# Turning gathered rows by TensorE in halves of 64 rows instead of blocks of 128

## The chip, the cores and the metric

One core of one Trainium2 chip runs the whole program. The metric is the device time of one execution in microseconds (us), lower is better; the time quoted for a kernel is the median of its runs. A profile of one execution stands beside the times. Its engines are PE (TensorE matmul), PEld (TensorE loading its stationary operand), DVE (VectorE), ACT (ScalarE), POOL (GpSimd) and SP (SyncE, which issues DMAs).

## The reference

Two stages in float32. The first is an attention of 8 batches of 8 heads, 576 positions, head size 64: a coarse attention over averages of 4 positions, repeated 4 times, plus a local attention in a band of 7 positions. Its output is laid out as 4608 tokens of 512 values. The second is a mixture of 8 experts with one expert for each token:

```python
def _moe_ref(x, modality_id, w_gate, modality_bias, w1, w2):
    logits = x @ w_gate + modality_bias[modality_id]      # x: 4608 x 512
    e_idx = np.argmax(logits, axis=1)
    ...                                                   # gate_w: softmax value of the chosen expert
    for e in range(8):
        mask = e_idx == e
        h = np.maximum(x[mask] @ w1[e], 0.0)              # 512 -> 1024
        out[mask] = gate_w[mask, None] * (h @ w2[e])      # 1024 -> 512
```

## The kernel before, in words

**Attention and routing.** The first part computes attention in an order written out by hand (a table of phases), stores the tokens' rows to a scratch tensor `xs` in HBM, and writes each token's number into a table `tab` sorted by expert. It fills about the first 260 us and the change doesn't touch it.

**Units of work.** The second part goes over a list `order` of units. A unit is up to 512 slots of one expert: blocks of 128 rows, H of them. There are two early units (H = 4, number 0 and 1, already prepared during the attention), six more of H = 4, one of H = 2, one of H = 1 and one of H = 2: 37 blocks in all. A loop for whatever is left (`For_i`) runs zero times with this data.

**What one unit does.** `gather` fetches the unit's rows from `xs` by indirect DMAs on POOL's queue into a buffer `R` (tile `xg`, 128 rows x 512 values for each block; two buffers in turn). `xsplit` turns each block: four transposes on TensorE, each of 128 rows x 128 columns against an identity matrix, fill one bank of PSUM (tile `xt`, tag `"T"`, three banks for all users of that tag). ACT then copies the bank to `xh` in the rounded matmul format, and DVE subtracts `xh` from the bank to get the remainder `xl`. `compute` runs the first layer as products of three kinds (`wh*xh`, `wh*xl`, `wl*xh`) on L886 and splits the hidden values into `hh` and `hl` on ACT and DVE; `second` runs the second layer block by block on L934, scales on ACT (L937) and scatters rows to the output with an indirect DMA on POOL (L938). Weights arrive by SP's queue and are split on ACT (L811) and DVE (L817).

**The order around the change.** `xsplit` is a generator: each `next` issues one step (the transposes of a block, then the copy, then the subtraction). While unit i is in its second layer, `mid(h)` at the head of each block calls `split(i + 1, h)`, which takes three `next` for each block it has to do; `SPLIT[4] = (2, 1, 1)` puts two blocks at the first `mid`, one at the second and one at the third. For unit 0 the steps are placed by hand inside the attention. Outside the hand-written part a scheduler sets the order on each engine: it follows the program's order but lets a later instruction go ahead where it expects an engine to be free. Both `xh` and `xl` have one buffer, so their copies begin only when the first layer of the unit before has read them.

Of the kernel before, what the change touches and what calls it, by code (L numbers as in the profile page):

```python
# [7 lines left out]
F32 = mybir.dt.float32  # L8
# [4 lines left out]
ALU = mybir.AluOpType  # L13
# [4 lines left out]
B, H, S, D = 8, 8, 576, 64  # L18
# [28 lines left out]
TB, SB = 3, 3  # L47
# [708 lines left out]
class Moe:  # L756
# [91 lines left out]
        s.turn["h"] = s.turn.get("h", -1) + 1  # L848
        return [s.xb.tile([128, 8, 512], F32R, name=nm) for nm in ("hh", "hl")]

    def xsplit(s, R, H=2):

        nc, C = s.nc, s.C
        xh = s.we.tile([128, 4, 512], F32R, name="xh")
        xl = s.we.tile([128, 4, 512], F32R, name="xl")
        for h in range(H):
            p = s.ps.tile([128, 4, 128], F32, name="xt", tag="T", bufs=TB)
            for k in range(4):
                nc.tensor.transpose(p[:, k, :], R[:, h, 128 * k : 128 * k + 128], C.ident)
            yield xh, xl  # L860
            hs = slice(128 * h, 128 * h + 128)
            nc.scalar.copy(xh[:, :, hs], p)
            yield
            nc.vector.tensor_tensor(xl[:, :, hs], p, xh[:, :, hs].bitcast(F32), op=ALU.subtract)
            yield
        return xh, xl
# [80 lines left out]
def build(tc, q, k, v, mid, w_gate, bias, w1, w2, out):  # L947
    nc = tc.nc
    with ExitStack() as ctx:
# [3 lines left out]
        ps = ctx.enter_context(tc.tile_pool(name="ps", bufs=2, space=PSUM))  # L953
        xs = dp.tile([NTOK + 1, DM], F32, name="xs")
        tab = dp.tile([NSLOT + CAP, 2], I32, name="tab")
        C = Consts(tc, cp, ps)
        moe = Moe(tc, ctx, C, ps, xs, tab, w1, w2, out)
        with ExitStack() as actx:
# [85 lines left out]
            def piece(key, f, done):  # L1044

                try:
                    next(going[key] if key in going else going.setdefault(key, f()))
                except StopIteration as x:
                    done(x.value)

            def split(u):
                piece(("x", u), lambda: moe.xsplit(E[u][2], 4), E[u].append)

            def wload(c):
                raw.append(moe.wload(E[0][0], c // 4, c % 4))
# [14 lines left out]
            T, R, E, W = {}, {}, {}, []  # L1070
# [28 lines left out]
            for j in range(13):  # L1099
                call(free + 0.4 + 0.15 * j, split, 0)  # L1100
# [65 lines left out]
        for i, (_, _, H) in enumerate(order):  # L1166
            if i == 0:
                with tc.high_priority():
                    lists["p"] = ro.pairs(cnt, moe.xp)
            if i == 1:  # L1170
                lists["m"] = ro.late(cnt, moe.xp)
            if i:
                gather(i + 2)

            def mid(h):
                if i == h == 0:
                    gather(2)
                split(i + 1, h)

            if H == 1:  # L1180
                moe.compute_half(Ts[i], Ws[i], Xs[i], step, mid)
            else:
                moe.compute(Ts[i], Ws[i], Xs[i], H, step, mid)
# [5 lines left out]
        with tc.For_i(0, nu, 1) as iv:  # L1189
# [4 lines left out]
            T = moe.entries(te, 1)  # L1194
            R = moe.gather(T)
# [33 lines left out]
```

## Time and profile before

| | |
|---|---|
| time, median of 3 runs | 715.84 us (709.83 to 716.35) |
| the profiled execution's own time, its span | 716.96 us, 715.3 us |
| PE busy in the span | 662.0 us (93%), 7467 matmuls |
| DVE, ACT, POOL busy | 379.2 us, 358.7 us, 262.9 us |
| granted TensorE clock, mean | 0.974 |
| transposes of `xsplit` (L859) | 148, of 128 x 128 each |

In a row of the profile `xt<-ident,xg 128*128 128x128 f32` means: tile `xt` is written, `ident` streams through TensorE (the moving operand, 128 partitions x 128 columns) and `xg` is held in it (the stationary operand, 128 rows x 128 columns). In a timeline the first number is the start in us from the span's start, the second the time until the last of the merged instructions has ended, and `x12` says how many were merged. Matmuls are pipelined: one begins before the one ahead has ended, so what a matmul costs in a full stream is the distance from its start to the next start, not its duration.

### The profile page before, as it was taken

How to read it: one execution, taken by the hardware profiler on the slowest of the kernel's cores; microseconds unless marked ns; L12 is line 12 of the kernel's file. 1: busy time of each engine (PE TensorE's matmuls, PEld its weight loads, DVE VectorE, ACT ScalarE, POOL GpSimd, SP SyncE). 2: the span in 40 equal slices, each digit the busy share in tenths (PEclk: the TensorE clock that was granted, in tenths of full speed). 3: DMA queues.
4: the chain of work that ended last, by engine and by line, in shares of the span. 5: the costliest groups of instructions: out<-in, count | busy, mean ns of one | idle time of the engine just before them, and what ended most of it. 6: DMA issues, size and time to landing. Idle time of an engine off the chain costs nothing. (4 is left out here: it accounts for less than half of the span.)

```text
span 715.3 us, 19216 instructions
## 1 busy us (share of the span) xinstructions
PE 662.0 (93%) x7467; PEld 535.7 (75%) x7467; DVE 379.2 (53%) x877; ACT 358.7 (50%) x804; POOL 262.9 (37%) x351
## 2 busy tenths in 40 slices
PE   7889999998968798999999999999999999999991
PEld 4677776776746666887888888888888888889790
DVE  3678687787848686836533245333453243525510
ACT  3678777777756574534444234433444234444610
POOL 6756665857647857353030310403103011010200
PEclk9799999999989899999999999999999999999996
DMA  9799799897889757579560744516435154346400
GB/s 178 148 186 173 162 165 181 174 184 130 145 147 214 152 151 186 154 228 294 143 219 21 189 148 116 179 58 190 165 102 156 67 162 148 103 133 186 159 13 29
DMA packets 179439, 107.93 MB, mean 151 GB/s; under 512 B 139309, under 2 KB 157777, under 8 KB 179346
## 3 DMA queue, kind: packets, MB, share of 16 engines
q1 hardware_dynamic: 172274, 87.49, 53.1%
q0 software_dynamic: 7072, 19.18, 8.3%
q8 instruction: 60, 0.98, 0.7%
q14 instruction: 33, 0.27, 0.2%
HBM read 87.39 MB, written 19.51 MB: 149 GB/s over the span
## 5 line engine op out<-in xcount | busy, mean ns | idle before, releaser
L938 POOL DMA_INDIRECT out_dram<-o,tg x37 | 40.9, 1106 | 302.7 <-ACT o L937 245.5
L817 DVE TENSOR_TENSOR wlo<-raw,whi 128x1024 fp32r<-128x1024 f32 x73 | 87.4, 1222 | 84.4 <-ACT whi L811 74.4
L891 DVE SCALAR_TENSOR_TENSOR hl<-l,hh 128x512 fp32r<-128x512 f32 x72 | 49.4, 688 | 101.7 <-ACT hh L890 101.7
L934 PE MATMUL l<-whi,hh 128*128 128x512 f32 x256 | 100.2, 395 | 0.0
L934 PE MATMUL l<-wlo,hh 128*128 128x512 f32 x256 | 99.6, 390 | 0.0
L934 PE MATMUL l<-whi,hl 128*128 128x512 f32 x256 | 99.6, 390 | 0.0
L890 ACT ACTIVATE hh<-l 128x512 fp32r<-128x512 f32 x72 | 42.9, 597 | 110.7 <-PE l L886 109.3
L886 PE MATMUL l<-xh,whi 128*128 128x512 f32 (+1 forms) x256 | 95.0, 374 | 0.4 <-DVE hl L891 0.2
L886 PE MATMUL l<-xh,wlo 128*128 128x512 f32 (+1 forms) x256 | 94.8, 370 | 0.0
L886 PE MATMUL l<-xl,whi 128*128 128x512 f32 (+1 forms) x256 | 94.7, 370 | 0.0
L811 ACT CAST whi<-raw 128x1024 fp32r<-128x1024 f32 x70 | 71.4, 1050 | 28.2 <-DMA raw<-in_moe_w_dram 18.2
L937 ACT ACTIVATE o<-l,tg 128x512 f32<-128x512 f32 x37 | 25.3, 687 | 98.5 <-PE l L934 70.5
L407 ACT COPY Pw<-lt 32x288 f32<-32x288 f32 x128 | 54.6, 426 | 3.2 <-DVE lt L402 1.8
L934 PEld LDWEIGHTS l<-wlo,hh 128*128 128x128 f32 x256 | 48.1, 188 | 10.1
L886 PEld LDWEIGHTS l<-xh,whi 128*128 128x128 f32 x256 | 48.1, 188 | 9.7 <-POOL xg L1063 0.5
L934 PEld LDWEIGHTS l<-whi,hl 128*128 128x128 f32 x256 | 48.1, 188 | 9.5
L934 PEld LDWEIGHTS l<-whi,hh 128*128 128x128 f32 x256 | 48.1, 188 | 9.5
L886 PEld LDWEIGHTS l<-xh,wlo 128*128 128x128 f32 x256 | 48.3, 189 | 8.3
L886 PEld LDWEIGHTS l<-xl,whi 128*128 128x128 f32 x256 | 48.3, 189 | 8.0
L337 PE MATMUL sc<-kT,qT 64*24 64x32 f32 x3072 | 45.5, 195 | 8.1 <-issue 7.4
L391 POOL TENSOR_TENSOR le<-le,zr 128x384 f32<-128x384 f32 x32 | 26.8, 836 | 70.0 <-DVE zr L387 53.5
L337 PEld LDWEIGHTS sc<-kT,qT 64*24 64x24 f32 x3072 | 35.3, 101 | 22.8 <-issue 18.2
(241 smaller groups left out, 1277.9 us busy)
## 6 DMA issues: line engine op xcount, KB each, us to landing
raw<-in_moe_w_dram SPq DMA_DIRECT2D x176, 128.0 KB
raw<-in_moe_w_dram SPq DMA_DIRECT2D x44, 512.0 KB
vw<-in_v_dram SPq DMA_DIRECT2D x53, 192.0 KB
qt<-in_q_dram SPq DMA_DIRECT2D x30, 288.0 KB
kt<-in_k_dram SPq DMA_DIRECT2D x30, 288.0 KB
xs<-R SPq DMA_DIRECT2D x64, 128.0 KB
vw<-in_v_dram SPq DMA_DIRECT2D x15, 96.0 KB
xs<-R SPq DMA_DIRECT2D x12, 64.0 KB
```

What stands on the lines that cost most here:

```text
L337: s.nc.tensor.matmul(p[32 * j : 32 * j + SUB, i, :], qT[r, q0 : q0 + SUB], kT[r, q0 : q0 + WIN], start=False, stop=(i == NB - 1), skip_gro ...
L391: s.nc.gpsimd.tensor_tensor(e, e, z[:, : 2 * NB].unsqueeze(2).broadcast_to([128, 2 * NB, WIN]), op=ALU.mult)
L407: s.nc.scalar.copy(s.Pw[n % NPW][r, :, j, :SUB], s.t["lt", n][r, :, :SUB])
L811: (nc.gpsimd.tensor_copy if turn <= 4 else nc.scalar.copy)(hi, raw)
L817: (nc.gpsimd if turn == 4 else nc.vector).tensor_tensor(lo, raw, hi.bitcast(F32), op=ALU.subtract)
L886: nc.tensor.matmul(p[:, f % n, :], a[:, fs], x[:, k, :N], start=(k == 0 and i == 0), stop=(k == 3 and i == 2))
L890: nc.scalar.activation(hh[:, g, :N], p, AF.Relu)
L891: nc.vector.scalar_tensor_tensor(hl[:, g, :N], p, 0.0, hh[:, g, :N].bitcast(F32), op0=ALU.max, op1=ALU.subtract)
L934: nc.tensor.matmul(p, a[:, f, hs], x[:, f % 2, :], start=(f == 0 and i == 0), stop=(f == 7 and i == 2))
L937: nc.scalar.mul(o, p, T[:, h, 1:2].bitcast(F32))
L938: nc.gpsimd.indirect_dma_start(out=s.out[:, :], out_offset=bass.IndirectOffsetOnAxis(ap=T[:, h, 0:1], axis=0), in_=o, in_offset=None, boun ...
```

## The change

All units but number 0 (which gets `pairs=False`) with an even H take two blocks at a time. Each block is turned in two halves: the lower 64 rows (r = 0) and the upper 64 rows (r = 1), so a transpose has a stationary operand of 64 rows x 128 columns and streams 64 columns of the identity. Sixteen such transposes are issued for the two blocks with lower and upper in turn; all lower halves of both blocks go to one bank of PSUM and all upper halves to another. The copy on ACT and the subtraction on DVE then take one bank each as before, 128 x 512 values, read and written with a stride in runs of 64. The number of steps of the generator for two blocks stays six: all sixteen transposes belong to the first.

```diff
-    def xsplit(s, R, H=2):
+    def xsplit(s, R, H=2, pairs=True):
         nc, C = s.nc, s.C
         xh = s.we.tile([128, 4, 512], F32R, name="xh")
         xl = s.we.tile([128, 4, 512], F32R, name="xl")
+        if pairs and H % 2 == 0:
+            for h in range(0, H, 2):
+                ps = [s.ps.tile([128, 2, 4, 64], F32, name="xt", tag="T", bufs=TB) for r in range(2)]
+                for g in range(2):
+                    for k in range(4):
+                        for r in range(2):
+                            rs = slice(64 * r, 64 * r + 64)
+                            nc.tensor.transpose(ps[r][:, g, k], R[rs, h + g, 128 * k : 128 * k + 128], C.ident[rs, rs])
+                for r in range(2):
+                    yield xh, xl
+                    p = ps[r].rearrange("m g k x -> m k g x")
+                    hi, lo = [x[:, :, 128 * h : 128 * h + 256].rearrange("m k (g r x) -> m k g r x", g=2, r=2)[:, :, :, r]
+                              for x in (xh, xl)]
+                    nc.scalar.copy(hi, p)
+                    yield
+                    nc.vector.tensor_tensor(lo, p, hi.bitcast(F32), op=ALU.subtract)
+                    yield
+            return xh, xl
         for h in range(H):
...
             def split(u):
-                piece(("x", u), lambda: moe.xsplit(E[u][2], 4), E[u].append)
+                piece(("x", u), lambda: moe.xsplit(E[u][2], 4, False), E[u].append)
```

## The prediction, made before the changed kernel was run

> **What bounds the kernel now.** I first read the busy times of the page, then the table of stretches of the expert part, with a cut at the last matmul.
>
> ```profile
> PE 662.0 (93%) x7467; PEld 535.7 (75%) x7467; DVE 379.2 (53%) x877; ACT 358.7 (50%) x804; POOL 262.9 (37%) x351
> ```
> ```profile
> core 0: us, PE busy (x) PEld busy (x) DVE busy (x) ACT busy (x) POOL busy (x), PEclk, DMA share, GB/s
> 284.00:340.00 56.00, 55.45 (x260) 45.47 (x261) 36.04 (x94) 26.14 (x35) 20.43 (x17) 1.00 0.78 230
> 340.00:460.00 120.00, 120.00 (x554) 99.53 (x553) 48.68 (x63) 47.66 (x66) 22.64 (x23) 1.00 0.48 138
> 600.00:699.00 99.00, 97.46 (x530) 84.46 (x529) 38.32 (x43) 38.41 (x52) 11.50 (x10) 1.00 0.38 120
> 699.00:715.30 16.30, 0.64 (x3) 0.19 (x1) 0.00 (x0) 0.69 (x1) 0.98 (x1) 0.58 0.04 16
> ```
>
> From 340 to 460 us PE is busy 120.00 of 120.00 at the full granted clock, while DVE and ACT are at 40%. Over these stretches it is idle for 0.5 to 1.5 us at most; behind the last matmul 16 us of closing work follow that the change doesn't touch. So a nanosecond of PE time added or taken in the second part moves the end by one, and the question is what the transposes cost on PE before and after. Next come the transposes' own line, and the matmuls around one batch.
>
> ```profile
> L859 PEld LDWEIGHTS xt<-ident,xg x148: 137/141/144, 262.5 to 671.6; 128*128 128x128 f32 x148
> L859 PE MATMUL xt<-ident,xg x148: 270/272/330, 262.5 to 671.7; 128*128 128x128 f32 x148
>   POOL xg L838: 7.6, 4
> ```
> ```profile
> 446.66 0.39 PE L934 MATMUL l<-wlo,hh 128*128 128x512 f32 x1
> ...
> 447.34 0.39 PE L934 MATMUL l<-wlo,hh 128*128 128x512 f32 x1
> 447.58 1.47 PE L859 MATMUL xt<-ident,xg 128*128 128x128 f32 x12
> 448.80 0.48 PE L934 MATMUL l<-whi,hh 128*128 128x512 f32 x1
> 449.12 0.40 PE L934 MATMUL l<-whi,hl 128*128 128x512 f32 x1
> ```
>
> Twelve transposes in 1.47 us, the last lasting 0.27: a step of (1.47 - 0.27) / 11 = 0.109 us. Products step by (447.34 - 446.66) / 3 = 0.227. From 447.34 to 449.12 are 1.78 us; less two product steps the batch costs 1.33, that is 12 x 0.109 and 0.02 for entering and leaving. Of the 148 transposes 16 are unit 0's and 4 the one-block unit's; the other 128 cost 128 x 0.109 = 14.0 us. That is all there is to win from.
>
> What sets the 0.109?
>
> ```profile
> 38.06 0.49 PE L413 MATMUL pdt<-ident,de 128*96 128x128 f32 x3
> 441.09 0.49 PE L859 MATMUL xt<-ident,xg 128*128 128x128 f32 x3
> ```
> ```profile
> 38.39 0.22 PEld L274 LDWEIGHTS tp<-ident,qt 128*128 128x128 f32 x2
> 38.39 0.25 PE L328 MATMUL sc<-mask,identb 128*128 128x192 bf16 x1
> 38.47 0.60 PE L274 MATMUL tp<-ident,qt 128*128 128x128 f32 x4
> ```
>
> Three transposes with 96 stationary columns take as long as three with 128, so the 128 streamed columns set the step. And a load of 128 columns that begins with the mask's matmul at 38.39 doesn't hold back its transpose at 38.47: it hides within 0.08 us.
>
> **What the change does to PE.** *Stream.* A half streams 64 columns: 0.109 x 64/128 = 0.055, call it 0.056 us. If the lower and the upper half run side by side, a pair of halves costs 0.056 in place of 0.109. Rows of two matmuls side by side:
>
> ```profile
> L364 PE MATMUL scd<-kd,qd 64*64 64x144 f32 x384 | 31.2, 296 | 0.4 <-POOL pool L112 0.4
> 35.13 0.95 PE L364 MATMUL scd<-kd,qd 64*64 64x144 f32 x12
> ```
>
> Twelve in 0.95 us less 0.28 for the last leave 0.67 us for five steps of two, about 0.12 a step when the entry is taken off; twelve one after the other would need 1.4. Those twelve differ in rows and in columns of the array, while the new halves share the columns. So full overlap isn't shown, and that is a rival below. With it, 128 pairs save 128 x 0.053 = 6.8 us.
>
> *Entering and leaving the half-row shape.* This is what the change adds and the diff doesn't show. Matmuls whose stationary operand has another count of rows or columns stand beside each other in the attention:
>
> ```profile
> 39.34 0.25 PE L328 MATMUL sc<-mask,identb 128*128 128x192 bf16 x1
> 39.52 0.25 PE L180 MATMUL mp<-ident,mf 36*128 36x36 f32 x1
> 39.70 0.29 PE L337 MATMUL sc<-kT,qT 64*24 64x32 f32 x12
> ```
> ```profile
> 270.96 0.96 PE L886 MATMUL l<-xh,whi 128*128 128x512 f32 x3
> 271.85 0.72 PE L442 MATMUL avl<-Pw,vw 128*64 128x96 f32 x12
> 272.50 0.50 PE L886 MATMUL l<-xl,whi 128*128 128x512 f32 x1
> 272.83 0.39 PE L886 MATMUL l<-xh,wlo 128*128 128x512 f32 x1
> ```
>
> The same mask matmul that let a full transpose follow after 0.08 lets the 36-row transpose of L180 follow after 0.18: 0.10 us for a change of rows alone. Into L442 the last product starts at 270.96 + 0.96 - 0.39 = 271.53, and 0.32 follow instead of 0.227: 0.09. Out of it: the last starts at 271.85 + 0.72 - 0.25 = 272.32 and 0.18 follow instead of 0.08, 0.10 again; then 0.33 instead of 0.227, another 0.10, since the first load could not be hidden. On the way in that uncovered load costs 0.06 (330 against 272 ns in L859's row). A run of halves between products thus pays 0.09 + 0.06 + 0.10 + 0.10 = 0.35 us; today's runs pay 0.02; net 0.33. If the loads were hidden after all it would be 0.2, and the sum below +1.2.
>
> The Trainium skill, page "TensorEngine Tiling (Array Packing)", section "Tiling Modes", says that changing the tiling mode drains TensorE. The rows above agree, with 0.10 us at each change; a price it doesn't give.
>
> *How many runs.* Each contiguous run of transposes would pay that. In the trace they stand from the first to the last of these rows in 27 runs, the one-block unit left out:
>
> ```profile
> 284.15 0.63 PE L859 MATMUL xt<-ident,xg 128*128 128x128 f32 x4 [1.84 <-DMA xg<-xs,tg]
> 422.80 0.27 PE L859 MATMUL xt<-ident,xg 128*128 128x128 f32 x1
> 422.82 0.47 PE L886 MATMUL l<-xh,whi 128*128 128x512 f32 x1
> 670.69 0.48 PE L934 MATMUL l<-whi,hh 128*128 128x512 f32 x1
> 671.31 0.66 PE L859 MATMUL xt<-ident,xg 128*128 128x128 f32 x4
> ```
>
> A middle unit has three: one alone as a filler in the first layer (422.80), the rest of that block (441.09), and twelve at 447.58, which are its last block and, two banks ahead, the first two blocks of the next unit. I expect these places again: a filler, the second pair, and the next unit's first pair.
>
> *The banks.* A pair holds two of three banks. The first pair is turned a layer early; so the second finds one bank free, for its lower halves, and the upper ones wait until DVE has subtracted the first pair's bank. Whether that is in time:
>
> ```profile
> 441.20 1.87 DVE L864 TENSOR_TENSOR xl<-xt,xh 128x512 fp32r<-128x512 f32 x3
> 485.46 1.27 DVE L864 TENSOR_TENSOR xl<-xt,xh 128x512 fp32r<-128x512 f32 x2
> 486.48 0.49 PE L859 MATMUL xt<-ident,xg 128*128 128x128 f32 x3
> 531.77 0.60 PE L859 MATMUL xt<-ident,xg 128*128 128x128 f32 x4
> 531.88 1.88 DVE L864 TENSOR_TENSOR xl<-xt,xh 128x512 fp32r<-128x512 f32 x3
> ```
>
> A subtraction takes 0.68, so the bank comes free at 441.88 for a run at 441.09 (late), at 486.14 for 486.48 (in time), at 532.56 for 531.77 (late). Two of three are late; I take four of the seven units of four blocks. There the scheduler issues the lower halves alone, goes on with products and issues the upper ones later: one run more, and 8 pairs with nothing overlapped, which cost 2 x 0.056 against 0.109, as much as today.
>
> *Beside PE.* ACT and DVE keep one instruction for each bank of the same size, in runs of 64. Twice their time would still be covered by the second layer's matmuls (DVE 48.68 of 120 us busy). On POOL's queue `gather` waits for the last transpose that read its buffer (7.6 us in four waits); it moves by the length of a run, and the rows are fetched a unit ahead. Before the last unit's second block (671.31, 0.62 behind a product instead of 0.23) PE already waits 0.4 us and may again.
>
> *Sum.* 31 runs x 0.33 = +10.2; 96 overlapped pairs x 0.053 = -5.1; 32 others +0.1: **+5.2 us**. The profiled execution took 716.96 and would take 722.2; on the median of 715.84, which I forecast, **721.0 us**.
>
> **The rivals.** *All pairs overlap.* The banks are in time, 27 runs: +8.9 - 6.8 = +2.1, 717.9 us; were each of the 16 pairs in one run, 5.3 - 6.8 = -1.5, 714.3. For it: the unit at 486.48. Against it: the two late ones and the fillers.
>
> *The price of the change of shape is not paid.* Then 6.8 us are won: 709.0. Only a missing drain would do it, and the 0.18 ahead of L180, itself a transpose of fewer rows, speaks against it. The Trainium skill, page "TensorE: Matmul & The Clock Gate", section "Part 3: Packing small matmuls", gives the span of packed tiles as one matmul and about 4 ns for each tile more, with no price of entry. By that rule this rival would hold; no run here shows tiles that share columns.
>
> *The halves don't run side by side (slower).* Both need the whole 128 columns of the array. If a half only starts when the other has streamed, pairs cost 0.112 and nothing is won: +0.4 + 10.2 = +10.6, 726.4. If the load of 128 columns also shows, at its bound of 0.08, 256 x 0.08 - 14.0 + 10.2 = +16.7, 732.5. It decides as soon as a pair costs more than 0.08. For it: no row shows two such loads at once. Against it: L364's loads do overlap. The same Trainium skill page, section "LDWEIGHTS (loading the stationary operand)", lets the load's time go with the columns and not with the rows, 107 ns for 128 of them. An estimate by it for loads in line is 256 x 0.107 = 27 us instead of 14; the row at 38.47 bounds it lower.
>
> *PE waits for the bank.* The sixteen stay in order and PE stands still from 441.1 to 441.9, 0.8 us in four units: +2.1 + 3.2 = +5.3, 721.1. The same time by another road.
>
> **How the numbers follow.** Chances: forecast 0.42, all overlapped 0.25, halves in line 0.14, PE waiting 0.12, no price 0.07. The range, 713 to 728, leaves out "no price" (709) and the upper part of the halves in line (to 732.5), some 0.15 together. A change under 1% (7.2 us) can't be told from none by these runs. Faster by more takes the whole of "no price": 0.04. Slower by more is the halves in line, and the forecast with four or more further runs: 0.33. Within: 0.63.
>
> **What would show it.** A pair of halves stepping by 0.056 (two starts a few ns apart); 0.32 before and about 0.15, then 0.33 behind each run; about 31 runs, fewer or more moving the sum by a third of a microsecond each; lower halves alone where DVE was late; PE without idle time. Wrong would be: halves of one bank in line, more than 40 runs, or waits of PE on `xl` beyond a microsecond a unit.

## The result: 734.9 us, 2.9% slower, and outside the predicted range

The changed kernel took 734.9 us (732.93 to 736.34, four runs) beside 716.1 us (709.83 to 716.47) of the kernel before on the same chip: a ratio of 1.0289, 95% interval 1.0239 to 1.034. Forecast were 721.0 us, 713 to 728. The profiled execution of after took 734.4 us; its span is 732.4 us, its mean granted clock 0.978. Ratios here and below are of fast runs alone, so they can differ by a few thousandths from the quotient of the medians, which are of all runs.

The page of after, busy times, and its table of stretches with the last cut again behind the last matmul:

```profile
PE 680.4 (93%) x7595; PEld 535.9 (73%) x7595; DVE 380.0 (52%) x877; ACT 359.3 (49%) x804; POOL 264.4 (36%) x351
```
```profile
340.00:460.00 120.00, 120.00 (x567) 94.08 (x567) 45.90 (x60) 43.90 (x61) 22.59 (x22) 1.00 0.44 135
600.00:716.00 116.00, 114.08 (x614) 96.89 (x613) 43.85 (x47) 44.57 (x59) 15.02 (x13) 1.00 0.38 118
716.00:732.40 16.40, 0.77 (x4) 0.31 (x2) 0.00 (x0) 0.69 (x1) 0.98 (x1) 0.62 0.05 18
```

PE's busy time grew by 18.4 us (662.0 before), that of DVE and ACT by less than 1. From 340 to 460 us PE is still never idle and at full clock: it has more to do for the same products. The end behind the last matmul is as long as before.

How much more, unit by unit: I cut PE's timeline at the products (1872 in both kernels, 192 for a unit of four blocks); a period runs from a unit's first product to the next unit's, the last one to one product step behind the last product's start.

| period of unit, us | 0 | 1 | 2 | 3 | 4 | 5 | 6 | 7 | 8 | 9 | 10 |
|---|---|---|---|---|---|---|---|---|---|---|---|
| before | 50.72 | 46.85 | 45.88 | 45.41 | 45.27 | 45.50 | 45.41 | 41.94 | 24.46 | 14.35 | 22.74 |
| after | 56.09 | 49.00 | 48.10 | 48.01 | 47.61 | 48.10 | 48.01 | 44.67 | 23.71 | 15.31 | 22.74 |

The 192 products alone take 192 x 0.2267 = 43.53 us. A steady unit thus pays 1.88 us for its transposes before and 4.48 after. The table adds up to +22.8 us; the attention happened to be 5.7 us shorter in the profiled execution of after (first product at 265.25 instead of 270.96), which leaves the 17.1 between the two last matmuls. The medians differ by 18.8. The start of the second part varies by itself: in the twelve traces of this document the first product stands anywhere from 256.6 to 271.0 us, in a part that the change doesn't touch. So kernels are compared below by the periods of their units as well as by their times.

**Where they stand.** One steady unit on PE in after, from the timeline (L904 first layer, L952 second, L863 the halves):

```profile
426.37 0.39 PE L904 MATMUL l<-xh,wlo 128*128 128x512 f32 x1
426.69 0.28 PE L863 MATMUL xt<-ident,xg 64*128 64x64 f32 x2
426.89 0.50 PE L904 MATMUL l<-xh,whi 128*128 128x512 f32 x1
427.23 0.39 PE L904 MATMUL l<-xl,whi 128*128 128x512 f32 x1
...
432.58 0.27 PE L863 MATMUL xt<-ident,xg 64*128 64x64 f32 x1
...
435.72 0.27 PE L863 MATMUL xt<-ident,xg 64*128 64x64 f32 x1
...
441.59 0.52 PE L863 MATMUL xt<-ident,xg 64*128 64x64 f32 x10
...
447.03 0.58 PE L863 MATMUL xt<-ident,xg 64*128 64x64 f32 x6
447.54 0.50 PE L952 MATMUL l<-whi,hh 128*128 128x512 f32 x1
447.98 0.33 PE L863 MATMUL xt<-ident,xg 64*128 64x64 f32 x2
...
450.50 0.71 PE L863 MATMUL xt<-ident,xg 64*128 64x64 f32 x8
...
455.22 0.28 PE L863 MATMUL xt<-ident,xg 64*128 64x64 f32 x2
```

With two halves at 455.22, which already belong to the unit after that one, these are eight runs in a unit's period; before there were three. The first pair goes in crumbs, 12 and more products apart: two halves a layer early (as those at 455.22 are for the next one), then 2, 1 and 1 in the first layer, and the other ten at 441.59. The second pair goes as 6 + 2 lower halves, with one product between, and eight upper ones later. Over the whole kernel the 256 halves stand in 56 runs, 14 of them of a single half, and only 51 pairs start together.

**What a run costs.** 426.37 to 427.23 are 0.86 us; less two product steps, 0.41 for a run of one step: 0.32 ahead of it, 0.20 behind, then 0.34, where a product has 0.227. Ten halves at 441.59 last 0.52, eight of one kind at 450.50 last 0.71: (0.71 - 0.27) / 7 = 0.063 a step. All runs of the tied kernels below follow 0.344 us + 0.062 for each step, a pair side by side (3 ns apart in the records) or a half alone. For after this gives 56 x 0.344 + (51 + 154) x 0.062 = 32.0 us. The 128 whole transposes before took about 16.1, but that figure is summed from the gaps around their runs and so takes in the slightly longer steps of the products behind each run, which the 32.0 leave out. Summed in the same way for after, with the waits for late rows taken out, the difference is about +17.2, not +15.9.

**The other 5.6 us** of the 22.8 are waits and what follows them, most of it in unit 0's period:

```profile
278.06 0.43 PE L863 MATMUL xt<-ident,xg 64*128 64x64 f32 x4 [1.44 <-issue]
280.23 0.69 PE L863 MATMUL xt<-ident,xg 64*128 64x64 f32 x4 [1.74 <-DMA xg<-xs,tg]
280.84 0.79 PE L904 MATMUL l<-xh,whi 128*128 128x512 f32 x1
281.44 0.63 PE L904 MATMUL l<-xl,whi 128*128 128x512 f32 x1
```
```profile
280.80:285.60 4.80, 4.80 (x13) 3.79 (x12) 2.13 (x2) 0.86 (x2) 0.00 (x0) 0.50 0.96 281
```

Unit 1's first halves at 278.06 stand where the kernel before had its first whole rows: 12.8 us behind the first product, 13.2 before (284.15). What is new is that the eight lower halves need both blocks' rows at once. PE waits ahead of the first four, as before (the view names no releaser), and again for the second block's rows: 3.2 us in all against 1.84. Behind that the granted clock is 0.50 in the 4.8 us of the row, and the products step by 0.43 until 286.13. The Trainium skill, page "TensorE: Matmul & The Clock Gate", section "Part 1: The HAM clock gate (the "warmup" mystery)", says that the clock is halved after idleness and comes back after some 3.4 us of work. The trace agrees in kind, but the half clock lasts about 6 us from the second four halves on. Before's single wait of 1.84 was followed by full speed.

### The profile page after: what moved, and what is told of

Read it like the earlier page. It is cut to its first block, busy times and chain, and to the rows that moved or that the text cites. A ratio compares the mean times of both kernels' runs of the same rounds, so it can differ in the third digit from the quotient of the medians.

```text
span 732.4 us, 19459 instructions
## 1 busy us (share of the span) xinstructions
PE 680.4 (93%) x7595; PEld 535.9 (73%) x7595; DVE 380.0 (52%) x877; ACT 359.3 (49%) x804; POOL 264.4 (36%) x351
## 5 line engine op out<-in xcount | busy, mean ns | idle before, releaser
L952 PE MATMUL l<-whi,hh 128*128 128x512 f32 x256 | 102.1, 400 | 0.0
L952 PE MATMUL l<-whi,hl 128*128 128x512 f32 x256 | 100.4, 393 | 0.0
L952 PE MATMUL l<-wlo,hh 128*128 128x512 f32 x256 | 99.8, 390 | 0.0
L904 PE MATMUL l<-xh,whi 128*128 128x512 f32 (+1 forms) x256 | 98.1, 386 | 0.8 <-DVE hl L909 0.8
L838 POOL DMA_INDIRECT xg<-xs,tg x37 | 40.2, 1087 | 157.3 <-PE xt L863 142.5
L904 PE MATMUL l<-xh,wlo 128*128 128x512 f32 (+1 forms) x256 | 95.8, 374 | 0.0
L904 PE MATMUL l<-xl,whi 128*128 128x512 f32 (+1 forms) x256 | 95.8, 374 | 0.0
L904 PEld LDWEIGHTS l<-xh,whi 128*128 128x128 f32 x256 | 48.7, 191 | 10.8 <-DVE hl L909 0.9
L952 PEld LDWEIGHTS l<-whi,hh 128*128 128x128 f32 x256 | 48.0, 188 | 10.8
L337 PE MATMUL sc<-kT,qT 64*24 64x32 f32 x3072 | 45.6, 195 | 11.0 <-issue 10.3
L952 PEld LDWEIGHTS l<-wlo,hh 128*128 128x128 f32 x256 | 48.1, 188 | 10.0
L904 PEld LDWEIGHTS l<-xh,wlo 128*128 128x128 f32 x256 | 48.8, 191 | 8.7
L952 PEld LDWEIGHTS l<-whi,hl 128*128 128x128 f32 x256 | 48.1, 188 | 9.6
L904 PEld LDWEIGHTS l<-xl,whi 128*128 128x128 f32 x256 | 49.0, 191 | 7.8
```

What stands on the lines that cost most here:

```text
L337: s.nc.tensor.matmul(p[32 * j : 32 * j + SUB, i, :], qT[r, q0 : q0 + SUB], kT[r, q0 : q0 + WIN], start=False, stop=(i == NB - 1), skip_gro ...
L838: nc.gpsimd.indirect_dma_start(out=R[:, h, :], out_offset=None, in_=s.xs[:n, :], in_offset=bass.IndirectOffsetOnAxis(ap=T[:, h, 0:1], axis ...
L904: nc.tensor.matmul(p[:, f % n, :], a[:, fs], x[:, k, :N], start=(k == 0 and i == 0), stop=(k == 3 and i == 2))
L952: nc.tensor.matmul(p, a[:, f, hs], x[:, f % 2, :], start=(f == 0 and i == 0), stop=(f == 7 and i == 2))
```

## The experiments

My theory after these two traces: the prices were as forecast and the number of runs wasn't, and more of the extra runs come from the crumbs in the first layer than from the banks. Rivals: pairs, steps and banks cost by themselves; the shortage of banks is the whole cause; waits for rows and weights are.

**whole_rows.** The changed kernel's steps, pairs and banks, but 128-row transposes:

```diff
-ps = [s.ps.tile([128, 2, 4, 64], F32, name="xt", tag="T", bufs=TB) for r in range(2)]
+ps = [s.ps.tile([128, 4, 128], F32, name="xt", tag="T", bufs=TB) for g in range(2)]
+for k in range(4):
+    for g in range(2):
+        nc.tensor.transpose(ps[g][:, k], R[:, h + g, 128 * k : 128 * k + 128], C.ident)
```

> The changed kernel's steps, pairs of blocks and two banks at a time, but each block is turned by four transposes of 128 rows, as before the change; 31 runs of transposes instead of 56. Theory (each contiguous run of half-row transposes pays 0.33 us for entering and leaving the shape, whole rows pay 0.02): 31 x 0.02 + 128 x 0.109, as before the change: 716.1 us, 714 to 718.5. Rival (the new order costs: both banks filled before the first copy, later copies, waits of PE for banks): most of the 18.8 us stays, over 725.

Measured 712.71 us beside 714.36 of the kernel before, ratio 0.9983 (0.9949 to 1.0017). It has 31 runs, as many as I had forecast for the halves, and its steady units take 45.4 to 45.6 us, as before. So with whole rows the two-block steps, their order and two banks at a time cost nothing that shows; the loss comes with the halves.

**one_run, two_runs, in_line.** The sixteen halves of a pair are tied in one run, the second pair two blocks later so that its banks are free; cut in two runs of eight; or tied with the eight lower halves ahead of the eight upper ones. The tie also holds the second layer's products in the order of the program:

```diff
+SPLIT = {4: (2, 0, 2), 2: (2,), 1: (2,)}              # one_run, in_line
+for g, k, r in [(g, k, r) for g in range(2) for k in range(4) for r in range(2)]:   # one_run
+for g, k, r in [(g, k, r) for r in range(2) for g in range(2) for k in range(4)]:   # in_line
+    with s.behind():      # ordered behind the product or half ahead of it
+        s.tail = nc.tensor.transpose(ps[r][:, g, k], ...)
```

> The half-row transposes of the change, with the sixteen of a pair tied into one run at the head of a block of the second layer (the second pair two blocks after the first): 16 runs instead of 56. Theory (price per run): 16 x 0.35 + 128 x 0.056 = 12.8 us of PE where before the change 27 x 0.02 + 128 x 0.109 = 14.5: 1.7 us under before, 714.4 us, 712.5 to 716.5. Rival (a half costs more by itself than half a transpose, or banks are waited for): over 722.

> As the one with one run per pair, but the sixteen transposes are cut into two runs of eight with a block of products between (15 pairs of 16): 31 runs. Theory (price per run 0.33 to 0.35 us): 15 x 0.35 = 5.2 us slower than with one run per pair, 719.6 us, 717.5 to 722. Rival (the number of runs is not what costs): within 1.5 us of the one with one run per pair.

> As the one with one run per pair, but all eight lower halves of a pair come first and then all eight upper ones, so that neighbours never lie in different rows. Theory (overlap is real and worth 0.053 us a pair): 128 x 0.056 = 7.2 us slower than the one with lower and upper in turn, 721.5 us, 719 to 724. Rival (the halves do not overlap anyway): the same time as that one.

Measured beside the same 714.36 us: one_run 717.28 us, ratio 1.0039 (1.0011 to 1.0067); two_runs 724.44, 1.0132 (1.0094 to 1.017); in_line 724.49, 1.0159 (1.0118 to 1.02). Runs of them, in this order, from their timelines:

```profile
492.52 0.39 PE L958 MATMUL l<-wlo,hh 128*128 128x512 f32 x1
492.84 0.71 PE L865 MATMUL xt<-ident,xg 64*128 64x64 f32 x16
493.48 0.50 PE L958 MATMUL l<-whi,hh 128*128 128x512 f32 x1
493.81 0.39 PE L958 MATMUL l<-whi,hl 128*128 128x512 f32 x1
```
```profile
501.69 0.46 PE L867 MATMUL xt<-ident,xg 64*128 64x64 f32 x8
```
```profile
485.31 1.01 PE L865 MATMUL xt<-ident,xg 64*128 64x64 f32 x16
```

Four more pairs take 0.71 - 0.46 = 0.25 us: 0.062 a pair. From 492.52 to 493.81 are 1.29; less two product steps 0.84, of which eight pairs are 0.50 and the run 0.344. Steady units: 45.25 us with two runs, 46.06 with four; summed, PE's gaps around the runs are 1.68 and 2.37 us a unit, 0.345 for each run more, and another 0.06 each in gaps between the products. That is the disputed price by itself. In line, a unit takes 45.85: 0.3 us more for each run of sixteen, since most halves don't pair up. Over all periods that is 4.1 us more than one_run. The medians differ by the 7.2 that were expected, which is partly luck: the traced execution of in_line took 715.45 us, 9 under its median, because its first product stands at 256.61 (263.87 in one_run).

A tied steady unit beats the kernel before by 0.16 us, yet one_run loses 3 us as a whole, and all three stand 3 to 5 us above the middle of what was expected, though the kernel before took 1.7 us less here than where the expectations took it from: one_run's first two periods are 54.37 and 50.49 us against 50.72 and 46.85. Waits for rows and weights there are a rival that is half right. PE's wait in these periods, and what ACT does ahead of the first of them:

```profile
PE l L907 <- DVE hl L912: 7.4, 2, 3.9
284.62 1.04 ACT L811 CAST whi<-raw 128x1024 fp32r<-128x1024 f32 x1 [4.82 <-DMA raw<-in_moe_w_dram]
285.57 1.08 ACT L911 ACTIVATE hh<-l 128x512 fp32r<-128x512 f32 x2
```

The hidden values stand on ACT behind a cast that waits for weights. No kernel ties whole rows, so whether the halves or the tie bring these waits isn't shown.

**not_early.** After with one edge: no half ahead of the last product of the first layer.

```diff
+with s.tc.issue_after(s.tail.ins) if s.tail else ExitStack():   # s.tail: that product
     nc.tensor.transpose(ps[r][:, g, k], ...)
```

> The changed kernel with one order more: no half may start before the last product of the first layer of the unit ahead, so the scheduler can't scatter the first pair into that layer as fillers. Its text gives 26 runs in place of 56. Theory (the number of runs, 0.364 us each, is what was mis-sized): a steady unit then has three runs (16, 8, 8) and costs 3 x 0.364 + 24 steps x 0.062 = 2.6 us for its transposes, where the changed kernel showed 4.48 and the kernel before 1.88; so about 0.7 us a unit over the kernel before, 5 to 6 in all: 719 to 723 us, some 12 under the changed kernel. Rival (the loss sits in what surrounds the runs, the rows and the weights that come late): 730 or more, with the waits of the early units as they were. Rival (the products in the first layer lose their cover when the fillers go, and copies of the rows come late): PE would wait on xh or xl at the head of the second pair, over 724.

Measured 722.84 us beside 713.61 (as for the next three), ratio 1.0132 (1.007 to 1.0195), 26 runs. A steady unit in its timeline:

```profile
482.00 0.71 PE L864 MATMUL xt<-ident,xg 64*128 64x64 f32 x16
...
486.94 0.40 PE L864 MATMUL xt<-ident,xg 64*128 64x64 f32 x3
487.27 0.50 PE L954 MATMUL l<-whi,hh 128*128 128x512 f32 x1
487.71 0.52 PE L864 MATMUL xt<-ident,xg 64*128 64x64 f32 x5
...
491.13 0.70 PE L864 MATMUL xt<-ident,xg 64*128 64x64 f32 x8
```

The crumbs are gone, the unit takes 46.11 us (+0.70, as expected) and the ratio falls by 0.0157, 11 us: 1.90 of the 2.60 us that a steady unit had lost. The crumbs are the larger part of the loss. The second pair is still apart, 3 + 5 and 8. The first two periods stay long, 55.05 and 49.01 us; PE no longer waits for rows there, but 3.8 us for `hl`.

**fourth_bank.** After with the second pair's upper halves in a bank of another tag.

```diff
-ps = [s.ps.tile([128, 2, 4, 64], F32, name="xt", tag="T", bufs=TB) for r in range(2)]
+ps = [s.ps.tile([128, 2, 4, 64], F32, name="xt", tag="S" if h and r else "T", ...) for r in range(2)]
```

> The changed kernel with a fourth bank: the upper halves of a unit's second pair go to a bank of another tag, so they need not wait for the subtraction and can run beside the lower ones. The fillers of the first layer are left as they are; the text has 52 runs in place of 56. Theory (runs by fillers are the larger part of the loss): 4 runs x 0.364 + 56 overlapped pairs x 0.062 = 5 us less than the changed kernel, about 730 us, 13 to 15 over the kernel before. Rival (the shortage of banks is the cause of the loss): the whole loss goes, 718 to 721 us.

Measured 730.89 us, ratio 1.0254 (1.0191 to 1.0317): of after's excess only 0.0035 goes, which is within the intervals. In its timeline:

```profile
472.67 0.28 PE L864 MATMUL xt<-ident,xg 64*128 64x64 f32 x2
...
478.56 0.27 PE L864 MATMUL xt<-ident,xg 64*128 64x64 f32 x1
...
481.71 0.27 PE L864 MATMUL xt<-ident,xg 64*128 64x64 f32 x1
...
493.71 0.46 PE L864 MATMUL xt<-ident,xg 64*128 64x64 f32 x8
494.10 0.50 PE L953 MATMUL l<-whi,hl 128*128 128x512 f32 x1
494.76 0.46 PE L864 MATMUL xt<-ident,xg 64*128 64x64 f32 x7
```

Now the second pair runs side by side, and a steady unit takes 47.13 us, 0.88 less than after. The crumbs remain, and so do 1.72 of the 2.60 us that a steady unit had lost: the bank is the smaller cause. The first two periods are 3.1 us longer than after's, 2.2 of it by waits (us in total, times, longest):

```profile
PE xt L864 <- DMA xg<-xs,tg: 3.4, 2, 1.7
PE l L905 <- DVE rcnt L752: 2.8, 1, 2.8
```

The first are the rows of unit 1's two blocks again; the other is a count of the routing.

**one_run_unit and mixed.** All 32 halves of a unit in one run, with the fourth bank, in all units; then in the units 3 to 7 only, with whole rows elsewhere.

```diff
-SPLIT = {4: (2, 1, 1), 2: (2,), 1: (2,)}
+SPLIT = {4: (0, 4), 2: (2,), 1: (2,)}       # one_run_unit; in mixed for the units of TIED
+TIED = range(3, 8)                          # mixed
```

> All 32 halves of a unit of four blocks tied in one run, with the fourth bank, put at the head of the second layer's last block but one; 9 runs in all. Theory: a steady unit costs 0.364 + 16 x 0.062 = 1.36 us for its transposes, 0.5 less than in the kernel before (1.88), over five units -2.6; the first two and the last three units lose 4 to 7 us to waits on rows and weights as they did where sixteen were tied. Sum: 716 to 720 us, the steady units' period 44.9 us against 45.4. Rival (a run costs more the longer it is, or the bank of the other tag holds up the second layer): period at 45.4 or above.

> The kernel before for the units 0, 1, 2 and the last three, with whole rows; the units 3 to 7 with 32 halves tied in one run and the fourth bank. Theory (halves are worth it where the runs are few and nothing else is late): five units x (1.88 - 1.36) = -2.6 us against the kernel before, a ratio of 0.9964, steady units at 44.9 us. Rival (halves lose in any order, by waits on what the tied order brings late): ratio 1.000 or above.

Measured: one_run_unit 716.73 us, ratio 1.0015 (0.9966 to 1.0064); mixed 711.93, 0.9983 (0.9949 to 1.0018). First a unit's run in the timeline of one_run_unit and PE's longest wait in its early units (waiter, what it waited for, us in total, times, longest), then PE's wait near the end of the kernel before and of mixed, and the stretch behind the latter:

```profile
483.38 1.21 PE L867 MATMUL xt<-ident,xg 64*128 64x64 f32 x32
```
```profile
PE l L910 <- DVE hl L915: 2.9, 1, 2.9
```
```profile
PE ht L913 <- ACT o L910: 1.4, 1, 1.4
PE ht L939 <- ACT o L936: 4.1, 1, 4.1
```
```profile
658.60:664.20 5.60, 5.54 (x19) 4.84 (x20) 4.49 (x6) 3.10 (x6) 0.00 (x0) 0.50 0.12 48
```

Both have steady units of 44.90 us, as computed, 0.51 under the kernel before: the halves do win where they stand in one run. one_run_unit loses it in unit 0 and 1 (54.26 and 49.15). mixed keeps those near the times of before (50.78, 47.17) and loses 6 us in the last four units, where PE waits 4.1 us for the one-block unit's hidden values `o` (1.4 before), which stand on ACT behind casts of the last weights; then the clock is at half for 5.6 us.

**mixed_3to6, mixed_2to6.** As mixed, with `TIED = range(3, 7)` and `range(2, 7)`.

> As mixed, but unit 7's rows too are turned whole, so 32 halves tied in one run are left in the units 3 to 6 only. In mixed the steady units took 44.90 us against 45.41 of the kernel before, but the last four units took 6.1 us more, 2.7 of them a longer wait of TensorE behind the weights of the last unit and most of the rest the half clock granted after that wait. Theory (the tail's loss comes from unit 7's late, tied halves): the last four units are back at the times of the kernel before, 103.3 us from unit 7's first product on within 1 us, the four tied units give 2.0 us: ratio 0.997. Rival (the weights reach the tail no sooner, and any gain of the steady units is waited away there): the units 3 to 6 at 44.9 us, the last four at 105 us or more, ratio 1.000.

> As the one beside it, with unit 2 tied too: five runs of 32. Theory: one more unit gains 0.5 to 1.8 us (the kernel before pays 3.17 us for the transposes in unit 1's period, five runs with unit 0's late rows among them, a tied run 1.34), if unit 1 doesn't wait for weights: ratio 0.995 to 0.997. Rival: unit 1's period goes to 48.5 us or more by a wait on the weights' split, as in the kernel with all units tied (49.15 against 46.85), and the ratio to 1.000 or above.

Measured 710.87 us beside 712.13, ratio 0.9982 (0.9942 to 1.0022), and 713.25, 1.0002 (0.9965 to 1.0038). Their waits at that place:

```profile
PE ht L939 <- ACT o L936: 2.9, 1, 2.9
```
```profile
PE ht L939 <- ACT o L936: 2.8, 1, 2.8
```

The tied units keep their 44.90 us, but the last four periods add up to 107.7 us in mixed_3to6 and 106.6 in mixed_2to6 (103.5 before): the first one's rival held. Unit 1 of mixed_2to6 takes 47.53 us, so the 48.5 of its rival did not come, yet its unit 0 took 52.90 and nothing was won. No version is measurably faster than the kernel before. Why the last weights are later for PE in these kernels, when ACT's order there is the same, stays open; each has one trace.

## Why the prediction was wrong

- **PE is the bound; a nanosecond there is one at the end.** Right: +17.1 us at the last matmul, the same closing work.
- **Steps.** A pair was to cost 0.056 and cost 0.062; a lone half too. The halves do run side by side: the rival "in line" is out. By the Trainium skill's figure of about 4 ns for each further tile (page "TensorE: Matmul & The Clock Gate", section "Part 3: Packing small matmuls") the pair would start as it does, 3 ns apart. But the rival built on it, no price of entry, is out.
- **Price of a run.** Forecast 0.35 gross, measured 0.344, in all the tied kernels. The four parts read from foreign rows (0.09 + 0.06 in, 0.10 + 0.10 out) held.
- **"How many runs": this step failed.** 31 were forecast, 56 came; 96 pairs side by side, and 51 came. At the measured prices, 31 runs and 160 steps give 20.6 us, +4.5 against the 16.1 before, near the forecast's +5.2. The 25 further runs are 8.6 us and 45 further steps 2.8. I had assumed that the places stay ("a filler, the second pair, and the next unit's first pair"). But a filler is an instruction or two, and the change halves the instruction and hands over sixteen at once: the scheduler placed four crumbs where it had placed one filler. not_early, which forbids them, takes back 11 of the 19 us. The prediction did name "more than 40 runs" as what would make it wrong, and gave it no rival with a price.
- **"The banks".** Four of the seven units of four blocks were to have the second pair's upper halves apart; in all seven they stand in a run of their own, eight in line. And not because DVE was late in the trace:

```profile
445.69 1.28 DVE L871 TENSOR_TENSOR xl<-xt,xh 128x512 fp32r<-128x512 f32 x2
```

  Both banks of the first pair were free at 446.97, ahead of the lower halves at 447.03, and the upper ones still came at 450.50. The order on PE is fixed before the run by the scheduler's expected times; the traced times that I used decide only waits, and PE had none here. The rival "PE waits for the bank" is out for the same reason.
- **ACT and DVE hidden.** Right: their busy time is as before. POOL's waits on the transposes grew far beyond the length of a run, in the view of the tile's waits:

```profile
  POOL xg L838: 142.5, 5
```

  Instead of 7.6 us; but PE's only waits for rows are those of unit 0's period, so it cost nothing that shows.
- **No loss outside the runs.** Wrong by 5.6 us: most of it the second wait in unit 0's period, for the rows of unit 1's second block, and the half clock behind it. The prediction put such a wait at the last unit's second block.

The forecast's mechanism was right in sign and price, and it was "slower by over 1%" at a chance of 0.33.

## What to carry to other kernels

Half-row transposes among whole products cost by the contiguous run (0.344 us here) more than by the piece (0.062): price the run from any place where such shapes already meet, and then count the runs in the order that will really be issued. Where a scheduler fills gaps, smaller instructions mean more and smaller fillers; tie those that must stay together before judging the idea. And a gain on the bounding engine holds only where nothing else is due next: here 0.5 us a unit was won in the middle, and the waits for rows and weights at both ends used it up.

## Hardware that I had not expected

Halves of different rows don't have to start in the order of the program. In in_line the records of one run begin at 485.311, then 485.423, .485, .548 and .610 for the lower halves; a sixth begins at .616, and from .729 on two streams step side by side until .796, when one ends; the last start is 486.102. By its place the one at .616 is the first upper half, ninth in the program, ahead of the lower ones at .672, .735 and .796. The records bear this out: the one at .616 carries a wait on DVE's semaphore of its own, as a half would that waits until its bank is read, and only those at .796 and 486.102 raise PE's semaphore, as the last of eight does. The sixteen last 1.01 us instead of 15 x 0.062 + 0.27 = 1.20 one after the other. The Trainium skill, page "TensorE: Matmul & The Clock Gate", section "Part 3: Packing small matmuls — row/col tiling", has matmuls start and end strictly in order. The starts here speak against that, though which record is which half is inferred from the steps and the semaphores.
